# Two elementwise steps of a two-layer attention and MLP kernel move from VectorE to GpSimd, with new GpSimd durations in its planner

## The chip, the cores and the metric

The kernel runs on one core of a Trainium2 chip. The metric is the device time in microseconds (us). A core has five engines that run on their own and meet at semaphores: TensorE (PE in the profile, PEld for its weight loads), ScalarE (ACT), VectorE (DVE), GpSimd (POOL) and SyncE (SP, which issues the DMA transfers). Each engine runs its instructions in a fixed order.

## What is computed

Two rounds of the same pair of blocks, on 2048 tokens of 512 features, all in bfloat16. The first block is softmax attention with 32 heads of 16 features; the second is an MLP with 1376 hidden features and GELU. Each has a layer norm ahead of it and a residual around it.

```python
def _A_ref(x, wqkv, wo):
    H = 32; Dh = D // H
    q, k, v = qkv[0], qkv[1], qkv[2]
    scores = jnp.einsum("bhqd,bhkd->bhqk", q, k) * Dh ** -0.5
    p = _softmax(scores, axis=-1)
    o = jnp.einsum("bhqk,bhkd->bhqd", p, v)
    return o.transpose(0, 2, 1, 3).reshape(B, S, D) @ wo
...
x = A_x
x = x + _A_ref(_layernorm(x), A_wqkv, A_wo)
x = x + _B_ref(_layernorm(x), B_w1, B_b1, B_w2, B_b2)
x = x + _A_ref(_layernorm(x), A_wqkv, A_wo)
x = x + _B_ref(_layernorm(x), B_w1, B_b1, B_w2, B_b2)
```

## The kernel before

**Tiles.** The code calls the two attention blocks `L == 1` and `L == 3`; here they are the first and the second layer. A layer's queries are cut into units (`qc`): four of 512 tokens in the first layer; three of 512 and two of 256 in the second. Heads are taken in eight groups of four (`hg`). A segment is one unit with one head group. Its scores are computed as tiles of 128 keys by 512 queries, for one head each: 16 key blocks times 4 heads is 64 tiles. The first unit of each layer is done in two parts, since its keys are not all there at first: its segments are twice as many and shorter, and their parts are joined afterwards. There are 88 segments and, counted as 128x512, 4096 tiles.

**Scores to output.** For every tile PE multiplies keys and queries into a PSUM bank (L1470), some engine takes the exponential, and PE multiplies the result with the values (L1658), adding into one bank, `ACCB`; the values have a column of ones, so the sum of the exponentials comes out as a 17th row. There are two ways to the exponential. ACT does it on three or two banks at once (L1455, into `PT`). DVE does it by a bit trick: it adds a constant to the score and writes it as a 16-bit integer whose bits are read as bfloat16 (L1555, PSUM to `dp`), and then makes three shifted copies, two tiles at a time (L1588, `dp` to `dp`, in SBUF); each of the four goes through its own product with a weighted copy of the values (`vs`). Only 5 of the 16 key blocks (`DK`) may go DVE's way.

**End of a segment** (`job_segend`). DVE transposes the 17 rows from PSUM into one of two buffers `accT` (L1688) and takes the reciprocal of the denominators, `rv` (L1714). Then `ob`, the part of the output that belongs to this head group, is the product of `accT` and `rv` (L1723, on DVE). In the first unit of a layer, GpSimd first joins the two parts (L1701 in the first part, L1709 to L1712 in the second). When the eight segments of a unit are through, `ob` is transposed by DMA and goes on to the output projection, the MLP and, in the first layer, to the layer norm and the q, k and v of the second (`job_post`, `job_ffn`, `job_lnqkv`).

**Squares.** The softmax uses no maximum but a bound, from the norms of the queries and of the keys. `job_qkv_tile` therefore squares q and k of each token tile (L991) and sums the squares (L1015). In the first layer the squares of k for twelve tiles are done by GpSimd, the rest by DVE. In the second layer DVE squares q and k of a tile together, 128x1024 elements. The bound of a query is then worked out in five small steps by GpSimd (L1029 to L1033).

**What else GpSimd does.** It scales the queries of a segment (`QT`, L1196), makes the weighted values (`vs`, L1221), applies some layer norms (L891) and their small steps (L881 to L886).

**The order.** Nothing is ordered by hand. The Python program plays the whole kernel through before it is built: jobs hand tasks to `Sched`, each with a priority, the tiles that it reads and writes, and a duration in microseconds; `Sched` takes for each engine the best task that is ready and puts it at the end of that engine's stream. How many tiles go DVE's way comes out of this: `take_d` hands DVE a tile when its planned work is small enough. The planned durations thus set the order and the split, and the real ones decide what it costs. For some GpSimd operations the planner also adds a delay to the L1588s beside them (the last number of a task, 0.09 to 0.38). `Hint` holds six thresholds of the planner and a string, `ORDER`, that picks one of ten settings of them for every eight groups of tiles. At last `refill` puts products with zeros (L1359, L1361, L1363) into gaps of PE[...].

Of the kernel before, what the change touches and what calls it, by code (L numbers as in the profile page):

```python
# [14 lines left out]
ALU = mybir.AluOpType  # L15
# [492 lines left out]
class Hint:  # L508
    BASE = dict(D_IDLE=1.2, PV_LEAST=0.75, HOLD_LATE=0.4, PV_NEAR=0.7, LIN2=9, D_STEAL=0)
    MODES = (dict(), dict(D_IDLE=0.8), dict(D_IDLE=1.7), dict(PV_LEAST=0.6), dict(PV_LEAST=0.9), dict(HOLD_LATE=0.2), dict(HOLD_LATE=0.6), dict(PV_NEAR=0.4), dict(LIN2=0.9), dict(D_STEAL=1.0))  # L510
    STEP = 8
    ORDER = '0355550015621021500127723542380000551183094330404202738042440023535555121020004212005090903453421320027044075009578104471100282939255971103200420580357499912000'

    def mode(self, k):
        self.__dict__.update(self.BASE)
# [10 lines left out]
class Builder:  # L526
# [341 lines left out]
    def ln_group(self, tiles, slot, prio, eps1, eps0, shift):  # L868

        for i, tt in enumerate(tiles):  # L870
            c = 4 * slot + i
            s = yield ("get", "st")
            yield Task("dve", prio, [I(lambda e, s=s, tt=tt: e.bn_stats(out=self.st[:, s, :], in_=self.xres[:, tt, :]), [("x", tt)], [("st", s)], 0.65)])
            yield Task("dve", prio - 0.3, [I(lambda e, s=s, c=c: e.bn_aggr(out=self.mv[:, c, :], in_=self.st[:, s, :]), [("st", s)], [("mv", c)], 0.172)])
            self.S_.release("st", s)
        n = len(tiles)
        c0 = 4 * slot
        rs = self.rs[:, c0:c0 + n]
        var = self.mv[:, c0:c0 + n, 1]
        R = ("rs", slot)  # L880
        yield Task("pool", prio, [I(lambda e: e.tensor_scalar(out=rs, in0=var, scalar1=eps1, scalar2=eps0, op0=ALU.mult, op1=ALU.add), [("mv", c0 + i) for i in range(n)], [R], 0.2),  # L881
                                  I(lambda e: e.tensor_tensor(out=rs, in0=rs, in1=self.cneg[:, 0:n], op=ALU.pow), [R, ("cneg",)], [R], 0.45 + 0.15 * n)])
        if shift:
            nmr = self.nmr[:, c0:c0 + n]
            yield Task("pool", prio, [I(lambda e: e.tensor_tensor(out=nmr, in0=self.mv[:, c0:c0 + n, 0], in1=rs, op=ALU.mult), [R] + [("mv", c0 + i) for i in range(n)], [("nmr", slot)], 0.2),
                                      I(lambda e: e.tensor_scalar(out=nmr, in0=nmr, scalar1=-1.0, scalar2=None, op0=ALU.mult), [("nmr", slot)], [("nmr", slot)], 0.2)])  # L886

    def ln_apply(self, tt, slot, i, dst, dres, prio, eng="dve"):
        c = 4 * slot + i
        if eng == "pool":  # L890
            return Task("pool", prio, [I(lambda e: e.tensor_scalar(out=dst, in0=self.xres[:, tt, :], scalar1=self.rs[:, c:c + 1], scalar2=self.nmr[:, c:c + 1], op0=ALU.mult, op1=ALU.add),  # L891
                                         [("x", tt), ("nmr", slot), ("rs", slot)], [dres], 0.92, (), 0.09)])
        return Task("dve", prio, [I(lambda e: e.tensor_scalar(out=dst, in0=self.xres[:, tt, :], scalar1=self.mv[:, c, 0:1], scalar2=self.rs[:, c:c + 1], op0=ALU.subtract, op1=ALU.mult),
                                    [("x", tt), ("mv", c), ("rs", slot)], [dres], 0.395, (), "fast")])

# [20 lines left out]
    def job_qkv_tile(self, L, tt, slot, i, left, prio, what):  # L916
# [12 lines left out]
        qs = yield ("get", "qk")  # L929
# [57 lines left out]
        N = h1 - h0  # L987
        SR = [("sq", ss, k) for k in range(k0, k1)]
        sq = self.sqs(ss)[:, h0:h1, :]
        eng = "pool" if what == "kv" else "dve"  # L990
        yield Task(eng, prio, [I(lambda e: e.tensor_tensor(out=sq, in0=v4, in1=v4, op=ALU.mult), [("qk", qs, k) for k in range(k0, k1)], SR, 0.14 + 0.00845 * N if eng == "dve" else 1.04)])  # L991
        if "k" in what:
            yield Task("dve", prio, [self.norms(self.n2k[:, tt, :], ("n2k", tt), ss, 1)])
            S_.mark(("n2k", L, tt))
# [28 lines left out]
    def bound(self, x, y, a, c, ns, dst, RQ, RN, prio, eng):  # L1023

        yi, y = y.bitcast(I32), y.bitcast(F32)
        RA, RC, RY = ("qt1", ns), ("qt2", ns), ("qy", ns)
        pool = eng == "pool"
        yield Task("dve", prio, [I(lambda e: e.tensor_scalar(out=yi, in0=x.bitcast(I32), scalar1=-0.5, scalar2=RSQRT_MAGIC, op0=ALU.mult, op1=ALU.add), RN, [RY], 0.18)])
        yield Task(eng, prio, [I(lambda e: e.tensor_tensor(out=a, in0=x, in1=y, op=ALU.mult), RN + [RY], [RA], 0.25 if pool else 0.2)])  # L1029
        yield Task(eng, prio, [I(lambda e: e.tensor_tensor(out=c, in0=a, in1=y, op=ALU.mult), [RA, RY], [RC], 0.25 if pool else 0.2)])  # L1030
        yield Task(eng, prio, [I(lambda e: e.tensor_scalar(out=c, in0=c, scalar1=-0.5, scalar2=1.5, op0=ALU.mult, op1=ALU.add), [RC], [RC], 0.217 if pool else 0.2)])
        yield Task(eng, prio, [I(lambda e: e.tensor_tensor(out=a, in0=a, in1=c, op=ALU.mult), [RA, RC], [RA], 0.25 if pool else 0.2)])
        yield Task(eng, prio, [I(lambda e: e.tensor_scalar(out=dst, in0=a.rearrange("p (n o) -> p n o", o=1), scalar1=-MARG, scalar2=0.0, op0=ALU.mult, op1=ALU.add),  # L1033
                                    [RA], [RQ], 0.333 if pool else 0.2)])

    def job_first_tile(self, tt, slot, i, left, prio):

# [105 lines left out]
    def job_scl(self, L, part, prio):  # L1143

        S_ = self.S_
        n = 16 if part == 1 else (4 if L == 1 else 12)
        k = (L // 2) * 2 + part
        n0 = 0
        if n == 16:
            n0 = 12  # L1150
            yield ("keys", [("n2k", L, tt) for tt in range(n0)])
            yield Task("dve", 2.5, [I(lambda e: e.tensor_reduce(out=self.n2k[:, 16, :], in_=self.n2k[:, 0:n0, :].rearrange("p t h -> p h t"), axis=AX.X, op=ALU.max), [("n2k", tt) for tt in range(n0)], [("n2k", 16)], 0.1 + 0.034 * n0)])
        ts = list(range(n0, 17 if n0 else n))
        yield ("keys", [("consts",)])
        yield ("keys", [("n2k", L, tt) for tt in range(n)])
        s = yield ("get", "kmx")
        yield Task("dve", prio, [I(lambda e: e.tensor_reduce(out=self.nm[:, :], in_=self.n2k[:, ts[0]:ts[-1] + 1, :].rearrange("p t h -> p h t"), axis=AX.X, op=ALU.max), [("n2k", tt) for tt in ts], [("nm",)], 0.1 + 0.034 * len(ts))])
        b = yield ("get", "mb")
        yield Task("pe", prio, [I(lambda e, b=b: e.transpose(self.psbf(b)[0:32, 0:128], self.nm[:, :], self.ident[:, :]), [("nm",), ("ident",)], [("ps", b)], 0.1)])
        yield Task("dve", prio, [I(lambda e, b=b: e.tensor_reduce(out=self.kmx[:, 0:1], in_=self.psbf(b)[0:32, 0:128], axis=AX.X, op=ALU.max), [("ps", b)], [("kmx", 0)], 0.2)])  # L1160
        S_.release("mb", b)
        yield Task("pool", prio, [I(lambda e: e.tensor_tensor(out=self.kmx[:, 1:2], in0=self.kmx[:, 0:1], in1=self.chalf[0:32, :], op=ALU.pow), [("kmx", 0), ("chalf",)], [("kmx", 1)], 0.55)])
        yield Task("dve", prio, [I(lambda e: e.tensor_scalar(out=self.krhs[:, :], in0=self.mask8[:, :], scalar1=self.kmx[:, 1:2], scalar2=None, op0=ALU.mult), [("kmx", 1), ("mask8",)], [("krhs",)], 0.1)])
        b = yield ("get", "mb")
        yield Task("pe", prio, [I(lambda e, b=b: e.matmul(self.ps[:, b, 0:8], lhsT=self.sel[:, :], rhs=self.krhs[:, :], start=True, stop=True), [("sel",), ("krhs",)], [("ps", b)], 0.08)])
        yield Task("dve", prio, [I(lambda e, b=b: e.tensor_scalar(out=self.scl[:, k, :], in0=self.ps[:, b, 0:8], scalar1=self.onesm[:, 0:1], scalar2=None, op0=ALU.add), [("ps", b), ("onesm",)], [("scl", k)], 0.15)])
        S_.release("mb", b)
        S_.release("kmx", s)
        S_.mark(("scl", L, part))
# [511 lines left out]
    def job_segend(self, sg):  # L1681
# [33 lines left out]
        if L == 3 and qc == len(self.units[3]) - 1 and hg == 7:  # L1715
            ob = self.obl[:, :].rearrange("p (b r) -> p b r", r=32)
            yield Task("dve", 1.2, [I(lambda e: e.tensor_tensor(out=ob[:, :, 0:16], in0=T[:, :, 0:16], in1=rv.unsqueeze(2).broadcast_to([128, nb, 16]), op=ALU.mult), [RA, ("rv", a)], [("obl",)], 0.147 + 0.268 * W / 512)])
            S_.release("accT", a)
            yield Task("dve", 1.2, [I(lambda e: e.transpose(self.OT[:, 7, 0:W], self.obl[:, 0:W]), [("obl",)], [("OT", 7)], 0.17 + 0.53 * W / 512)])
        else:  # L1720
            if self.prev(L, qc):
                yield ("keys", [("obt",) + self.prev(L, qc)])
            yield Task("dve", 1.2, [I(lambda e: e.tensor_tensor(out=self.ob[:, 0:nb, hg, :], in0=T[:, :, 0:16], in1=rv.unsqueeze(2).broadcast_to([128, nb, 16]), op=ALU.mult), [RA, ("rv", a)], [("ob", hg)], 0.147 + 0.268 * W / 512)])  # L1723
            S_.release("accT", a)
        S_.mark(("ot", L, qc, hg))
        if L == 1 and qc == self.NC - 1:
# [292 lines left out]
```

## Time and profile before

The time is 1564.23 us, the median of three runs (1563.62 to 1565.77). The profiled execution spans 1564.7 us.

| Engine | Busy, us | Share of the span |
|---|---|---|
| PE | 1517.7 | 97% |
| ACT | 1517.1 | 97% |
| DVE | 1459.9 | 93% |
| POOL | 321.2 | 21% |

The largest groups: ACT's exponentials (L1455) 1433.7 us in 1273 instructions; DVE's first step (L1555) 638.1 us in 960, its shifted copies (L1588) 559.9 us in 1452. The multiplication that is moved (L1723) takes DVE 27.6 us in 71 instructions; the squares of the second layer (L991, 128x1024) 11.0 us in 16.

How to read the profile: a group's line has the source line, engine and operation, what is written and read with its shape, the count, then the busy time and the mean of one, and then the idle time of the engine just before these instructions and what ended it. An engine overlaps the end of one instruction with the start of the next, so that counts times means come out above busy times. In a table by windows the columns behind the length are the busy times of PE, PEld, DVE, ACT and POOL, each with its count, the granted clock of PE, and the share and GB/s of the DMA engines.

### The profile page before, as it was taken

The numbers are of one execution on the slowest core, as the hardware profiler recorded it, in microseconds if no ns is written. First come the engines' busy times: TensorE is split into PE (matmuls) and PEld (weight loads), VectorE is DVE, ScalarE is ACT, GpSimd is POOL, SyncE is SP. The second block draws the span as 40 slices with busy tenths as digits, with TensorE's granted clock in tenths as the row PEclk, the third lists the DMA queues.
The fourth block names the chain that finished last, engine by engine and source line by source line (L and its number), as shares of the span: only waits on it lengthen the run. The fifth ranks groups of instructions, "written<-read, shape, count | busy, mean of one in ns | idle before, by whom it ended". The sixth has DMA issues, their size and how long they took to land.

```text
span 1564.7 us, 39699 instructions
## 1 busy us (share of the span) xinstructions
PE 1517.7 (97%) x16674; PEld 483.1 (31%) x16674; DVE 1459.9 (93%) x3256; ACT 1517.1 (97%) x1361; POOL 321.2 (21%) x558
## 2 busy tenths in 40 slices
PE   9999999999999999999999999999999999999998
PEld 3222222232223222222222322222232232344444
DVE  7699999999999899989999799999899999999894
ACT  8979999999999999999999999999999999999996
POOL 3575312001210021203222227410001000020100
PEclk9999999999999999999999999999999999999999
DMA  7663111203311232223832232310102000211110
GB/s 162 116 143 97 35 31 32 61 17 85 85 40 46 47 76 59 61 48 92 145 45 66 56 82 63 62 25 22 35 16 44 22 17 25 41 45 32 43 30 19
DMA packets 212451, 88.69 MB, mean 57 GB/s; under 512 B 183307, under 2 KB 207152, under 8 KB 212272
## 3 DMA queue, kind: packets, MB, share of 16 engines
q1 hardware_dynamic: 212272, 86.16, 24.9%
q8 instruction: 130, 2.13, 0.6%
q14 instruction: 49, 0.40, 0.1%
HBM read 34.65 MB, written 19.48 MB: 35 GB/s over the span
## 4 chain that ended last, share of the span: by engine, by line
ACT 34%; DVE 33%; PE 29%; issue 2%; POOL 1%; SPq 1%; DMA 1%; POOLq 0%; DVEq 0%
ACT PT L1455 33%; DVE dp L1555 13%; DVE dp L1588 10%; PE ps L1470 9%; PE ps L1658 8%; PE ps L1835 3%; PE ps L1792 2%; PE ps L950 2%; DVE accT L1688 2%; DVE n L1015 1%; ACT h L1827 1%; PE ps L1359 1%; DVE sq L991 1%; DVE h L1816 1%; PE ps L1068 1%
## 5 line engine op out<-in xcount | busy, mean ns | idle before, releaser
L1455 ACT ACTIVATE PT<-ps 128x1536 bf16<-128x1536 f32 (+1 forms) x1273 | 1433.7, 1285 | 28.5 <-PE ps L1470 25.1
L1555 DVE TENSOR_SCALAR dp<-ps 128x512 uint16<-128x512 f32 x960 | 638.1, 679 | 36.7 <-PE ps L1470 34.2
L1470 PE MATMUL ps<-QT,KT 32*128 32x512 bf16 (+1 forms) x4608 | 599.1, 359 | 19.6 <-ACT PT L1455 6.8
L1588 DVE TENSOR_SCALAR dp<-dp 128x1024 uint16<-128x1024 uint16 (+1 forms) x1452 | 559.9, 427 | 4.6 <-PE ps L1658 1.6
L1658 PE MATMUL ps<-PT,V 128*17 128x512 bf16 (+1 forms) x3525 | 483.8, 358 | 0.2 <-ACT PT L1455 0.2
L1658 PE MATMUL ps<-dp,vs 128*17 128x512 bf16 (+1 forms) x3249 | 467.6, 357 | 0.9 <-DVE dp L1588 0.4
L1470 PEld LDWEIGHTS ps<-QT,KT 32*128 32x128 bf16 x4608 | 161.1, 91 | 545.9 <-ACT PT L1455 286.3
L1196 POOL TENSOR_SCALAR QT<-qraw,scl,qbias 128x512 bf16<-128x512 bf16 (+1 forms) x83 | 72.3, 872 | 764.6 <-PE ps L1470 758.1
L1658 PE MATMUL ps<-dp,V 128*17 128x512 bf16 (+1 forms) x1083 | 227.1, 358 | 1.6 <-DVE accT L1688 0.6
L1363 PE MATMUL ps<-zw 128*32 128x448 bf16 (+23 forms) x1808 | 172.2, 321 | 0.8 <-DVE dp L1555 0.7
L1658 PEld LDWEIGHTS ps<-dp,vs 128*17 128x17 bf16 x3249 | 119.1, 88 | 115.4 <-issue 87.2
L1658 PEld LDWEIGHTS ps<-PT,V 128*17 128x17 bf16 x3525 | 116.9, 88 | 92.8 <-issue 78.5
L1361 PE MATMUL ps<-zw 32*128 32x444 bf16 (+5 forms) x465 | 132.8, 317 | 0.0
L1359 PE MATMUL ps<-zw 128*128 128x448 bf16 (+17 forms) x487 | 114.7, 334 | 3.2 <-DVE onec L754 2.1
L1792 PE MATMUL ps<-yT,wf 128*128 128x512 bf16 (+3 forms) x396 | 101.7, 361 | 3.1 <-DVE dp L1588 1.3
L950 PE MATMUL ps<-wqkv,xnT 128*128 128x512 bf16 x336 | 93.4, 382 | 5.8 <-DVE dp L963 2.2
L1363 PEld LDWEIGHTS ps<-zw 128*32 128x32 bf16 x1808 | 62.5, 95 | 27.8 <-DVE dp L1555 4.6
L1658 PEld LDWEIGHTS ps<-dp,V 128*17 128x17 bf16 x1083 | 55.5, 88 | 41.4 <-issue 24.1
L1221 POOL TENSOR_SCALAR vs<-V 128x340 bf16<-128x340 bf16 (+2 forms) x72 | 61.8, 859 | 26.1 <-PE ps L1658 15.1
L1688 DVE STREAM_TRANSPOSE accT<-ps 128x512 f32<-128x512 f32 (+1 forms) x88 | 57.8, 657 | 7.1 <-PE ps L1658 7.0
L1816 DVE TENSOR_SCALAR h<-ps,b1c 128x512 bf16<-128x512 f32 (+2 forms) x88 | 61.9, 703 | 1.9 <-PE ps L1792 1.5
L1359 PEld LDWEIGHTS ps<-zw 128*128 128x128 bf16 x487 | 37.6, 98 | 64.7 <-issue 40.0
(182 smaller groups left out, 885.5 us busy)
## 6 DMA issues: line engine op xcount, KB each, us to landing
vs<-vs_scr SPq DMA_DIRECT2D x56, 255.0 KB, 2.7
wf<-in_B_w_dram SPq DMA_DIRECT2D x90, 128.0 KB, 2.9
q_scr<-qk SPq DMA_DIRECT2D x20, 256.0 KB, 2.1
k_scr<-qk SPq DMA_DIRECT2D x12, 256.0 KB, 2.0
out_dram<-xres SPq DMA_DIRECT2D x16, 128.0 KB, 1.8
vs_scr<-vs SPq DMA_DIRECT2D x8, 255.0 KB, 2.9
xres<-in_A_x_dram SPq DMA_DIRECT2D x7, 256.0 KB, 3.2
v_scr<-vst SPq DMA_DIRECT2D x12, 136.0 KB, 1.7
```

What stands on the lines that cost most here:

```text
L950: yield Task("pe", prio if c0 == 0 else min(prio, HINT.LIN2), [I(lambda e, c=c: e.matmul(self.ps[:, b, :], lhsT=xnT[:, c, :], rhs=self.wqk ...
L1359: fn = lambda e: e.matmul(self.ps[:, b, 0:w], lhsT=self.zw[:, 0:128], rhs=self.zw[:, 0:w], start=st, stop=st, skip_group_check=True)
L1361: fn = lambda e: e.matmul(self.ps[:, b, 0:w], lhsT=self.zw[32 * p:32 * p + 32, 0:128], rhs=self.zw[32 * p:32 * p + 32, 0:w], start=st, sto ...
L1363: fn = lambda e: e.matmul(self.ps[32 * p:32 * p + 32, b, 0:w], lhsT=self.zw[:, 0:32], rhs=self.zw[:, 0:w], start=st, stop=st, skip_group_c ...
L1455: S_.submit(Task("act", 1e-5 * gi, [I(lambda e, pt=pt, n=n, b0=b0: e.activation(out=self.PT[:, pt:pt + n, :], in_=self.ps[:, b0:b0 + n, :] ...
L1470: return [I(lambda e, kb=kb, i=i: e.matmul(self.ps[:, b, i * W:(i + 1) * W], lhsT=self.KT[32 * hp:32 * hp + 32, hg, kb * 128:(kb + 1) * 12 ...
L1555: self.S_.submit(Task("dve", 0.0, [I(lambda e: e.tensor_scalar(out=self.dp[:, u, w * 512:(w + 1) * 512], in0=self.ps[:, b, :], scalar1=BIT ...
L1588: yield Task("dve", pr, [I(lambda e, k=k, v=v: e.tensor_scalar(out=self.dp[:, v, 0:N], in0=self.dp[:, u, 0:N], scalar1=float(SHIFT[k]), sc ...
L1658: ops.append((nth[j, sh] + 0.1 * i, I(lambda e, hp=hp, v=v, ap=ap[:, i * W:(i + 1) * W], first=first and i == 0, W=W: e.matmul(self.ps[32 ...
L1688: yield Task("dve", 0.3, [I(lambda e: e.transpose(self.accT[:, a, 0:W], self.ps[:, ACCB, 0:W]), [("ps", ACCB)], [RA], 0.17 + 0.535 * W / 5 ...
L1792: yield Task("pe", pr if c0 == 0 else min(pr, HINT.LIN2), [I(lambda e, c=c: e.matmul(self.ps[0:M, b, off:off + W], lhsT=self.w1(fc, c), rh ...
L1816: S_.submit(Task("dve", pr - 0.7, [I(lambda e, fc=fc, M=M, b=b: e.tensor_scalar(out=hv[0:M, fc * W:(fc + 1) * W], in0=self.ps[0:M, b, 0:W] ...
```

## The change

The multiplication by the reciprocal denominators, L1723 (L1724 after the change), goes to GpSimd, all but the two of the last unit for head groups 5 and 6 (head group 7 of that unit has a line of its own, L1717, and stays on DVE). The squares of the second layer go to GpSimd for the twelve token tiles below 12. Both are meant to free DVE, which is then to take more of the exponentials. The planner gets durations for GpSimd's small operations that are nearer to those of the trace, and the string `ORDER` is another one.

```diff
-    ORDER = '0355550015621021500127723542380000551183094330404202738042440023535555121020...'
+    ORDER = '500550000942402210717323201145450083900431778210649440584538550402055502101004...'
...
-        ... op0=ALU.mult, op1=ALU.add), [("mv", c0 + i) for i in range(n)], [R], 0.2),
-        ... in1=self.cneg[:, 0:n], op=ALU.pow), [R, ("cneg",)], [R], 0.45 + 0.15 * n)])
+        ... op0=ALU.mult, op1=ALU.add), [("mv", c0 + i) for i in range(n)], [R], 0.28),
+        ... in1=self.cneg[:, 0:n], op=ALU.pow), [R, ("cneg",)], [R], 0.58 + 0.15 * n)])
...
-        eng = "pool" if what == "kv" else "dve"
-        ... SR, 0.14 + 0.00845 * N if eng == "dve" else 1.04)])
+        eng = "pool" if what == "kv" or L == 3 and tt < 12 else "dve"
+        ... SR, 0.14 + 0.00845 * N if eng == "dve" else 1.04 * N / 32)])
...
-            yield Task("dve", 1.2, [I(lambda e: e.tensor_tensor(out=self.ob[:, 0:nb, hg, :], in0=T[:, :, 0:16], in1=rv.unsqueeze(2).broadcast_to([128, nb, 16]), op=ALU.mult), [RA, ("rv", a)], [("ob", hg)], 0.147 + 0.268 * W / 512)])
+            late = L == 3 and qc == len(self.units[3]) - 1 and hg > 4
+            yield Task("dve" if late else "pool", 1.2, [I(lambda e: e.tensor_tensor(out=self.ob[:, 0:nb, hg, :], in0=T[:, :, 0:16], in1=rv.unsqueeze(2).broadcast_to([128, nb, 16]), op=ALU.mult), [RA, ("rv", a)], [("ob", hg)], 0.147 + 0.268 * W / 512 if late else 0.1 + 0.58 * W / 512)])
```

The other GpSimd durations changed: layer norm's shift 0.2 and 0.2 to 0.24 and 0.43, its application 0.92 to 0.99; the bound's five steps 0.25, 0.25, 0.217, 0.25, 0.333 to 0.34, 0.26, 0.27, 0.29, 0.45; the square root of the key bound 0.55 to 0.7.

More of the change, by code (lines that the diff above doesn't have):

```diff
@@ L511 @@
     STEP = 8
-    ORDER = '0355550015621021500127723542380000551183094330404202738042440023535555121020004212005090903453421320027044075009578104471100282939255971103200420580357499912000'
+    ORDER = '500550000942402210717323201145450083900431778210649440584538550402055502101004030404145325972120344000190229570058123013000773000079300003010022814735200804803'
     def mode(self, k):
@@ L880, in ln_group @@
         R = ("rs", slot)
-        yield Task("pool", prio, [I(lambda e: e.tensor_scalar(out=rs, in0=var, scalar1=eps1, scalar2=eps0, op0=ALU.mult, op1=ALU.add), [("mv", c0 + i) for i in range(n)], [R], 0.2),
-                                  I(lambda e: e.tensor_tensor(out=rs, in0=rs, in1=self.cneg[:, 0:n], op=ALU.pow), [R, ("cneg",)], [R], 0.45 + 0.15 * n)])
+        yield Task("pool", prio, [I(lambda e: e.tensor_scalar(out=rs, in0=var, scalar1=eps1, scalar2=eps0, op0=ALU.mult, op1=ALU.add), [("mv", c0 + i) for i in range(n)], [R], 0.28),
+                                  I(lambda e: e.tensor_tensor(out=rs, in0=rs, in1=self.cneg[:, 0:n], op=ALU.pow), [R, ("cneg",)], [R], 0.58 + 0.15 * n)])
         if shift:
             nmr = self.nmr[:, c0:c0 + n]
-            yield Task("pool", prio, [I(lambda e: e.tensor_tensor(out=nmr, in0=self.mv[:, c0:c0 + n, 0], in1=rs, op=ALU.mult), [R] + [("mv", c0 + i) for i in range(n)], [("nmr", slot)], 0.2),
-                                      I(lambda e: e.tensor_scalar(out=nmr, in0=nmr, scalar1=-1.0, scalar2=None, op0=ALU.mult), [("nmr", slot)], [("nmr", slot)], 0.2)])
+            yield Task("pool", prio, [I(lambda e: e.tensor_tensor(out=nmr, in0=self.mv[:, c0:c0 + n, 0], in1=rs, op=ALU.mult), [R] + [("mv", c0 + i) for i in range(n)], [("nmr", slot)], 0.24),
+                                      I(lambda e: e.tensor_scalar(out=nmr, in0=nmr, scalar1=-1.0, scalar2=None, op0=ALU.mult), [("nmr", slot)], [("nmr", slot)], 0.43)])
     def ln_apply(self, tt, slot, i, dst, dres, prio, eng="dve"):
@@ L891, in ln_apply @@
             return Task("pool", prio, [I(lambda e: e.tensor_scalar(out=dst, in0=self.xres[:, tt, :], scalar1=self.rs[:, c:c + 1], scalar2=self.nmr[:, c:c + 1], op0=ALU.mult, op1=ALU.add),
-                                         [("x", tt), ("nmr", slot), ("rs", slot)], [dres], 0.92, (), 0.09)])
+                                         [("x", tt), ("nmr", slot), ("rs", slot)], [dres], 0.99, (), 0.09)])
         return Task("dve", prio, [I(lambda e: e.tensor_scalar(out=dst, in0=self.xres[:, tt, :], scalar1=self.mv[:, c, 0:1], scalar2=self.rs[:, c:c + 1], op0=ALU.subtract, op1=ALU.mult),
@@ L989, in job_qkv_tile @@
         sq = self.sqs(ss)[:, h0:h1, :]
-        eng = "pool" if what == "kv" else "dve"
-        yield Task(eng, prio, [I(lambda e: e.tensor_tensor(out=sq, in0=v4, in1=v4, op=ALU.mult), [("qk", qs, k) for k in range(k0, k1)], SR, 0.14 + 0.00845 * N if eng == "dve" else 1.04)])
+        eng = "pool" if what == "kv" or L == 3 and tt < 12 else "dve"
+        yield Task(eng, prio, [I(lambda e: e.tensor_tensor(out=sq, in0=v4, in1=v4, op=ALU.mult), [("qk", qs, k) for k in range(k0, k1)], SR, 0.14 + 0.00845 * N if eng == "dve" else 1.04 * N / 32)])
         if "k" in what:
@@ L1028, in bound @@
         yield Task("dve", prio, [I(lambda e: e.tensor_scalar(out=yi, in0=x.bitcast(I32), scalar1=-0.5, scalar2=RSQRT_MAGIC, op0=ALU.mult, op1=ALU.add), RN, [RY], 0.18)])
[L1029 to L1032, printed above, removed]
+        yield Task(eng, prio, [I(lambda e: e.tensor_tensor(out=a, in0=x, in1=y, op=ALU.mult), RN + [RY], [RA], 0.34 if pool else 0.2)])
+        yield Task(eng, prio, [I(lambda e: e.tensor_tensor(out=c, in0=a, in1=y, op=ALU.mult), [RA, RY], [RC], 0.26 if pool else 0.2)])
+        yield Task(eng, prio, [I(lambda e: e.tensor_scalar(out=c, in0=c, scalar1=-0.5, scalar2=1.5, op0=ALU.mult, op1=ALU.add), [RC], [RC], 0.27 if pool else 0.2)])
+        yield Task(eng, prio, [I(lambda e: e.tensor_tensor(out=a, in0=a, in1=c, op=ALU.mult), [RA, RC], [RA], 0.29 if pool else 0.2)])
         yield Task(eng, prio, [I(lambda e: e.tensor_scalar(out=dst, in0=a.rearrange("p (n o) -> p n o", o=1), scalar1=-MARG, scalar2=0.0, op0=ALU.mult, op1=ALU.add),
-                                    [RA], [RQ], 0.333 if pool else 0.2)])
+                                    [RA], [RQ], 0.45 if pool else 0.2)])
     def job_first_tile(self, tt, slot, i, left, prio):
@@ L1161, in job_scl @@
         S_.release("mb", b)
-        yield Task("pool", prio, [I(lambda e: e.tensor_tensor(out=self.kmx[:, 1:2], in0=self.kmx[:, 0:1], in1=self.chalf[0:32, :], op=ALU.pow), [("kmx", 0), ("chalf",)], [("kmx", 1)], 0.55)])
+        yield Task("pool", prio, [I(lambda e: e.tensor_tensor(out=self.kmx[:, 1:2], in0=self.kmx[:, 0:1], in1=self.chalf[0:32, :], op=ALU.pow), [("kmx", 0), ("chalf",)], [("kmx", 1)], 0.7)])
         yield Task("dve", prio, [I(lambda e: e.tensor_scalar(out=self.krhs[:, :], in0=self.mask8[:, :], scalar1=self.kmx[:, 1:2], scalar2=None, op0=ALU.mult), [("kmx", 1), ("mask8",)], [("krhs",)], 0.1)])
```

## The prediction

> **What bounds the kernel now.** I read the page's totals first, then the busy time of each engine by query unit (the windows end where a unit's last `ob` multiplication starts), then what ScalarE (ACT, whole run) and VectorE (DVE, between 160 and 1525 us) waited for, then the groups by shape, and last the timeline where GpSimd (POOL) and DVE meet.
>
> ```profile
> PE 1517.7 (97%) x16674; PEld 483.1 (31%) x16674; DVE 1459.9 (93%) x3256; ACT 1517.1 (97%) x1361; POOL 321.2 (21%) x558
> ...
> 423.00:608.00 185.00, 182.44 (x1807) 53.34 (x1795) 178.59 (x396) 184.31 (x161) 26.64 (x49) 1.00 0.24 57
> 608.00:797.00 189.00, 185.63 (x1846) 54.90 (x1847) 183.75 (x403) 185.16 (x161) 37.49 (x54) 1.00 0.37 77
> ```
>
> ACT is nearly full and DVE close behind. In the two units shown (first layer, qc 2 and 3; the columns after the length are PE, PEld, DVE, ACT, POOL) ACT is idle 0.7 and 3.8 us, DVE 6.4 and 5.2 us. PE is as busy, but it has about 420 us of L1359, L1361 and L1363, which are filler products with zeros, so it is not the bound. POOL is idle four fifths of the time: its work is free unless it disturbs others.
>
> ```profile
> ACT PT L1455 <- PE ps L1470: 25.1, 47, 6.3
> ...
> DVE dp L1555 <- PE ps L1470: 29.8, 48, 2.1
> ...
> L1455 ACT ACTIVATE PT<-ps 128x1536 bf16<-128x1536 f32 x590 | 893.9, 1515 | 20.2 <-PE ps L1470 17.3
> L1455 ACT ACTIVATE PT<-ps 128x1024 bf16<-128x1024 f32 x683 | 731.8, 1086 | 8.3 <-PE ps L1470 7.7
> L1555 DVE TENSOR_SCALAR dp<-ps 128x512 uint16<-128x512 f32 x960 | 638.1, 679 | 36.7 <-PE ps L1470 34.2
> L1588 DVE TENSOR_SCALAR dp<-dp 128x1024 uint16<-128x1024 uint16 x1428 | 555.0, 430 | 4.6 <-PE ps L1658 1.6
> ```
>
> The exponentials of 4096 score tiles (128x512) are split: ACT does 590x3 + 683x2 = 3136 of them, DVE 960 by its bit trick. So DVE time that comes free can buy tiles from ACT, and ACT time is nearly the kernel's time. Pieces overlap in time: in the trace consecutive starts lie 1.331 us (three tiles) and 0.904 us (two tiles) apart on ACT, 0.601 us for L1555, 0.335 for L1588 at 1024 and 0.202 at 512. I use these distances below, since they are what an engine really spends. One tile on DVE costs 0.601 + 1.5 x 0.335 = 1.10 us.
>
> ```profile
> L1723 DVE TENSOR_TENSOR ob<-accT,rv 128x256 bf16<-128x256 f32 x56 | 23.4, 419 | 0.0
> ...
> L1723 DVE TENSOR_TENSOR ob<-accT,rv 128x128 bf16<-128x128 f32 x15 | 4.2, 281 | 0.0
> ...
> L1709 POOL TENSOR_TENSOR OT<-OT,dw 128x256 f32<-128x256 f32 x16 | 10.7, 667 | 24.4 <-ACT dw L1708 24.4
> L1712 POOL TENSOR_TENSOR accT<-accT,OT 128x256 f32<-128x256 f32 x16 | 12.0, 748 | 1.3
> ...
> L991 POOL TENSOR_TENSOR sq<-h x2: 1041/1042/1042, 56.8 to 80.4; 128x512 bf16<-128x512 bf16 x2
> ...
> 186.93 0.68 DVE L1555 TENSOR_SCALAR dp<-ps 128x512 uint16<-128x512 f32 x1
> 187.53 0.96 DVE L1588 TENSOR_SCALAR dp<-dp 128x1024 uint16<-128x1024 uint16 x1
> ...
> 187.48 0.73 POOL L1712 TENSOR_TENSOR accT<-accT,OT 128x256 f32<-128x256 f32 x1
> ```
>
> The last three lines carry the danger. An L1588 that starts 0.05 us after a two-input GpSimd operation takes 0.96 us instead of 0.42, while the L1555 beside it, which reads PSUM, keeps its 0.68.
>
> [...] L1588s blocked by an L1709 all run on from 0.485 us after it began (of its 0.62), those blocked by an L1712 from about 0.60 us (of 0.73). It also shows the other direction: an L1196 on POOL took 2.11 us behind five L1588s in a row, 0.77 without. [...]
>
> **The change part by part.** The counts come from comparing the two programs' instruction streams.
>
> 1. *Removed from DVE*: 56 `ob` multiplications at 512 queries (0.332 us apart in starts), 13 at 256 (0.199), 12 squares of 128x1024 (0.599): 18.6 + 2.6 + 7.2 = 28.4 us. The last two of the last unit stay (`late`).
> 2. *Added to DVE*: the scheduler spends the room on 16 more tiles: 976 L1555, 1443 + 42 L1588. 16 x 0.601 + 15 x 0.335 + 18 x 0.202 = 18.3 us.
> 3. *Removed from ACT*: 584 triples and 684 pairs, so -6 x 1.331 + 1 x 0.904 = -7.1 us. This is the gain. By unit, first layer qc 2 and 3 get 6 tiles more each, second layer qc 1 4 more, the rest within 2 of before.
> 4. *Added to POOL*: 56 x 0.7 + 13 x 0.4 + 12 x 2.08 (twice the 512 row) = 69 us, on an engine with 1240 us idle. Hidden as work.
> 5. *The lock*. In 40 of the 71 cases the DVE instruction after the reciprocal is an L1588. [...] Summing, for every L1709, how much the DVE instructions beside it exceeded their undisturbed median gives 0.22 us per operation; for L1712 0.27, for single-input bf16 L891 0.14. I take 0.22 for `ob` at 512 and half that at 256: 13.7 us. For the squares no such row exists at 1024 elements; two 0.4 us operations met a 512 square late and lost nothing or 0.02. A 2.08 us hold in which a fast instruction comes after some 0.7 us on average could cost over 1.2 us; the lowest is L891's 0.14. I take 0.8, so 9.6 us. Sum 23 us; ends 10 and 45.
> 6. *Net on DVE*: -28.4 + 18.3 + 23 = +13 us, to about 1473. In qc 2: -(8 x 0.332 + 4 x 0.599) + 6 x 1.10 + 8 x 0.22 + 4 x 0.8 = +6.5 us against 6.4 idle. In qc 3 the same against 5.2. These units become DVE-bound and lose most of ACT's 2 x 2.7 us if the lock costs what I take; elsewhere there is room. A late tile does not all show, as DVE work of the post stages can slide. I charge 2.4 of the 5.3 us.
> 7. *The new wait*: `ob` now stands in POOL's fixed order, in 43 of 69 cases behind a `QT` (0.93 us), sometimes before L1709 or L1221. Behind the waiting `ob` are the next `QT` (needed a segment later), and the release of `accT`, of which there are two, so the transposition of the next but one segment waits. Segments last 20 us mostly; only in second layer part 1 (950 to 1000) 4 to 8 us, where POOL is 33.4 of 50 busy and gets 6 more. I charge nothing, at most 2 us.
> 8. *New POOL durations in the planner, new `ORDER`*: these only move instructions. The start (ACT idle 8 us between 80 and 120) and the filler count (108 matmuls fewer with the 48 more P·V products) may go either way: +-4 us, mean nothing.
>
> Sum: 1564.2 - 7.1 + 2.4 = 1559.5.
>
> **Rivals.** (a) *The lock hardly bites*: DVE's extra is at its low end, +0.2 us net, ACT's gain comes in full and some of its 14.1 us of waits in the middle goes: 1564.2 - 7.1 - 3 = 1554. For it: POOL mostly starts behind a running L1588, and two thirds of the kernel is not near DVE's limit. Against: L1709's 0.22 is measured under the same conditions. (b) *The lock eats the gain*: qc 2 and 3 gain nothing (5.3 back), the shorter stages lose another 1: 1563.5, no difference. For it: the sums in 6. (c) *Slower*: squares block for 1.8 us each, `ob` for 0.38 (L1712 beside a fast operation), DVE +35 us net. The planner does not count this, so PE's in-order stream stands at tiles that are late (L1470 already waits 66.7 us for L1555) and ACT runs dry: a third of 35 us beyond the 7.1 gained, 1564.2 - 7.1 + 12 = 1569. Against: DVE has 50 us idle between 160 and 1520.
>
> **How the numbers follow.** Forecast 1559.5: 0.4. (a) 0.2; (b) 0.2; (c) 0.2. Faster by over 0.2% (below 1561.1): the first two, less a little of the first's upper edge: 0.58. Same 0.21, slower 0.21. Range 1550 to 1570: from (a) with 4 us of luck in the order to (c).
>
> **What would show it.** Right: L1455 near 584 + 684 with ACT busy about 7 us less; L1723's successor on POOL at 0.62 to 0.75 us; mean of L1588 up from 430 to about 445 ns; DVE idle in qc 2 and 3 below 3 us. Wrong: L1588's mean unchanged (then a), ACT waits for L1470 above 35 us (then b or c), a longer wait of L1688 or L1658 around 950 to 1000 (then step 7), a stretch of low PE clock, or a start that is longer or shorter by more than 4 us (then step 8).

## The result, and the profile after

The changed kernel takes 1582.2 us (median; 1580.35 to 1582.89), against 1563.92 us beside it: 1.0113 times the time before, 95% interval [1.0095, 1.013]. It is 18 us slower, where 4.7 us faster was forecast, and lies outside the range (1550 to 1570).

First the page of the changed kernel, then its groups by shape, then what ACT waited for in all, and its query units qc 2 and 3 of the first layer (columns as before: length, PE, PEld, DVE, ACT, POOL, PE clock, DMA share, GB/s).

```profile
PE 1502.0 (95%) x16439; PEld 480.0 (30%) x16566; DVE 1477.1 (93%) x3224; ACT 1513.9 (96%) x1356; POOL 377.1 (24%) x639
```

```profile
L1455 ACT ACTIVATE PT<-ps 128x1536 bf16<-128x1536 f32 x584 | 876.5, 1501 | 37.4 <-PE ps L1470 34.7
L1455 ACT ACTIVATE PT<-ps 128x1024 bf16<-128x1024 f32 x684 | 724.7, 1075 | 9.2 <-PE ps L1470 8.6
L1555 DVE TENSOR_SCALAR dp<-ps 128x512 uint16<-128x512 f32 x976 | 647.7, 678 | 38.1 <-PE ps L1470 34.8
L1588 DVE TENSOR_SCALAR dp<-dp 128x1024 uint16<-128x1024 uint16 x1443 | 583.6, 445 | 4.2 <-PE ps L1658 0.7
...
L1724 POOL TENSOR_TENSOR ob<-accT,rv 128x256 bf16<-128x256 f32 x56 | 36.8, 658 | 153.7 <-DVE rv L1714 152.0 <-DVE dw L1707 1.4 <-DMA xnT<-xn 0.3
...
L991 POOL TENSOR_TENSOR sq<-qk 128x1024 bf16<-128x1024 bf16 x12 | 23.1, 1924 | 23.1 <-DVE qk L963 23.1
```

```profile
ACT PT L1455 <- PE ps L1470: 43.3, 77, 5.5
```

```profile
426.00:620.00 194.00, 184.34 (x1791) 51.56 (x1800) 185.65 (x399) 186.59 (x162) 36.65 (x56) 0.98 0.22 53
620.00:812.00 192.00, 182.29 (x1860) 54.30 (x1878) 188.74 (x402) 184.21 (x159) 48.63 (x72) 1.00 0.39 78
```

The work moved as counted: 16 tiles went from ACT to DVE, and ACT is busy 3 us less. DVE is busier than before, by 17 us, though 28 us were taken from it and 18 added. ACT's waits for scores grew by 18 us (25.1 to 43.3); less the 3 us, that is nearly the 15.9 us between the two traces. By unit, from the start of one unit's last transposition (L1688) to that of the next, in the two traces and in two of the experiments below:

| Stage | before | changed | e1: squares short | e3: both short |
|---|---|---|---|---|
| layer 1, qc 1 | 187.9 | 189.6 | 185.3 | 184.6 |
| layer 1, qc 2 | 185.7 | 192.7 | 187.1 | 186.2 |
| layer 1, qc 3 | 189.4 | 193.3 | 188.5 | 188.7 |
| all else | 1001.7 | 1005.0 | 1005.6 | 1000.6 |
| span | 1564.7 | 1580.6 | 1566.6 | 1560.1 |

Of the 15.9 us between the two traces, 12.6 lie in three units. Each of the three holds four of the twelve squares. In these units ACT waited 18.7 us for scores, where it had waited 4.7 us before.

This is one square, the sixth and the costliest of the twelve, in the timeline of the changed kernel: first POOL, then DVE, then PE's weight loads and products, then ACT.

```profile
591.67 0.25 POOL L1032 TENSOR_TENSOR qt<-qt 128x32 f32<-128x32 f32 x1
591.88 1.89 POOL L991 TENSOR_TENSOR sq<-qk 128x1024 bf16<-128x1024 bf16 x1
```

```profile
591.48 0.67 DVE L977 CAST vst<-ps 128x512 bf16<-128x512 f32 x1
592.07 2.45 DVE L1588 TENSOR_SCALAR dp<-dp 128x1024 uint16<-128x1024 uint16 x2
594.44 0.67 DVE L1555 TENSOR_SCALAR dp<-ps 128x512 uint16<-128x512 f32 x1
```

```profile
595.17 0.09 PEld L1470 LDWEIGHTS ps<-QT,KT 32*128 32x128 bf16 x1 [1.86 <-DVE dp L1555]
```

```profile
595.17 0.38 PE L1470 MATMUL ps<-QT,KT 32*128 32x512 bf16 x1 [1.57 <-DVE dp L1555]
...
597.14 0.61 PE L1470 MATMUL ps<-QT,KT 32*128 32x512 bf16 x3
```

```profile
589.66 5.76 ACT L1455 ACTIVATE PT<-ps 128x1024 bf16<-128x1024 f32 x5
597.80 2.51 ACT L1455 ACTIVATE PT<-ps 128x1536 bf16<-128x1536 f32 x2 [2.38 <-PE ps L1470]
```

The square starts 0.19 us before an L1588. That L1588 takes 1.99 us, and with the next one 2.45 us, where two undisturbed ones (0.42 us each, starts 0.335 us apart) take about 0.75. Behind them in DVE's order stands an L1555, which takes 0.67 us as elsewhere (the twelve L1555s that ran beside a square took 0.67 to 0.68 us), but comes 1.5 us late, as e1 will show; a score product of PE waits 1.9 us until it has ended and its bank is free (595.11), and everything behind that product in PE's order waits too. The products for the scores that ACT needs next start only at 597.14, and ACT stands for 2.38 us until they are done. By that time such a product takes 0.61 us instead of 0.38: PE's granted clock is at half from 595.9 to 602.7, right after five microseconds in which PE was busy for 3.61.

```profile
590.00:595.00 5.00, 3.61 (x34) 0.82 (x32) 5.00 (x8) 4.93 (x5) 4.07 (x6) 1.00 0.20 54
595.90:602.70 6.80, 6.32 (x38) 0.96 (x38) 4.95 (x12) 3.40 (x3) 1.52 (x5) 0.50 0.01 4
```

The half clock makes this square look worse than the rest, but it is not the cause of the loss. It comes once in this trace, and for about 3.4 us each in the trace of the kernel before (at 1214 us) and in that of the repeated run e9. The one run of the changed kernel whose granted clock was 1.0 took 1580.35 us.

### The profile page after: what moved, and what is told of

It is laid out like the page before. It is cut to its first block, busy times and chain, and to the rows that moved or that the text cites. A ratio compares the mean times of both kernels' runs of the same rounds, so it can differ in the third digit from the quotient of the medians.

```text
span 1580.6 us, 39479 instructions
## 1 busy us (share of the span) xinstructions
PE 1502.0 (95%) x16439; PEld 480.0 (30%) x16566; DVE 1477.1 (93%) x3224; ACT 1513.9 (96%) x1356; POOL 377.1 (24%) x639
## 4 chain that ended last, share of the span: by engine, by line
DVE 38%; PE 30%; ACT 27%; issue 3%; DMA 1%; SPq 1%; POOL 1%; POOLq 0%; another core or an unknown queue 0%; DVEq 0%
ACT PT L1455 24%; DVE dp L1555 15%; DVE dp L1588 14%; PE ps L1470 10%; PE ps L1658 9%; PE ps L1836 4%; PE ps L1793 3%; DVE accT L1688 1%; PE ps L950 1%; ACT h L1828 1%; PE ps L1359 1%; DVE n L1015 1%; DVE st L873 1%; PE ps L1363 1%; PE ps L1068 1%
## 5 line engine op out<-in xcount | busy, mean ns | idle before, releaser
L1455 ACT ACTIVATE PT<-ps 128x1536 bf16<-128x1536 f32 (+1 forms) x1268 | 1430.1, 1271 | 46.6 <-PE ps L1470 43.3
L1555 DVE TENSOR_SCALAR dp<-ps 128x512 uint16<-128x512 f32 x976 | 647.7, 678 | 38.1 <-PE ps L1470 34.8
L1470 PE MATMUL ps<-QT,KT 32*128 32x512 bf16 (+1 forms) x4608 | 612.5, 360 | 27.9 <-DVE dp L1555 13.5
L1588 DVE TENSOR_SCALAR dp<-dp 128x1024 uint16<-128x1024 uint16 (+1 forms) x1485 | 593.8, 441 | 4.4 <-PE ps L1658 0.9
L1658 PE MATMUL ps<-PT,V 128*17 128x512 bf16 (+1 forms) x3507 | 492.2, 359 | 0.0
L1196 POOL TENSOR_SCALAR QT<-qraw,scl,qbias 128x512 bf16<-128x512 bf16 (+1 forms) x83 | 69.4, 837 | 609.8 <-PE ps L1470 602.9
L1363 PE MATMUL ps<-zw 128*32 128x448 bf16 (+22 forms) x1695 | 162.7, 319 | 1.3 <-DVE dp L1555 1.1
L1361 PE MATMUL ps<-zw 32*128 32x444 bf16 (+4 forms) x469 | 135.6, 318 | 0.0
L1359 PE MATMUL ps<-zw 128*128 128x448 bf16 (+18 forms) x434 | 105.5, 338 | 3.9 <-DVE onec L754 2.1
L950 PE MATMUL ps<-wqkv,xnT 128*128 128x512 bf16 x302 | 87.3, 384 | 14.3 <-issue 3.3
L1793 PE MATMUL ps<-yT,wf 128*128 128x512 bf16 (+3 forms) x361 | 92.7, 357 | 6.7 <-issue 3.9
L1724 POOL TENSOR_TENSOR ob<-accT,rv 128x256 bf16<-128x256 f32 (+1 forms) x69 | 42.6, 617 | 199.5 <-DVE rv L1714 197.7
L1688 DVE STREAM_TRANSPOSE accT<-ps 128x512 f32<-128x512 f32 (+1 forms) x88 | 57.8, 657 | 11.8 <-PE ps L1658 11.5
```

The source lines that it names most:

```text
L950: yield Task("pe", prio if c0 == 0 else min(prio, HINT.LIN2), [I(lambda e, c=c: e.matmul(self.ps[:, b, :], lhsT=xnT[:, c, :], rhs=self.wqk ...
L1196: yield Task(eng, 0.4, [I(lambda e: e.tensor_scalar(out=self.QT[:, q, 0:W], in0=src, scalar1=self.scl[:, k, hg:hg + 1], scalar2=self.qbias ...
L1359: fn = lambda e: e.matmul(self.ps[:, b, 0:w], lhsT=self.zw[:, 0:128], rhs=self.zw[:, 0:w], start=st, stop=st, skip_group_check=True)
L1361: fn = lambda e: e.matmul(self.ps[:, b, 0:w], lhsT=self.zw[32 * p:32 * p + 32, 0:128], rhs=self.zw[32 * p:32 * p + 32, 0:w], start=st, sto ...
L1363: fn = lambda e: e.matmul(self.ps[32 * p:32 * p + 32, b, 0:w], lhsT=self.zw[:, 0:32], rhs=self.zw[:, 0:w], start=st, stop=st, skip_group_c ...
L1455: S_.submit(Task("act", 1e-5 * gi, [I(lambda e, pt=pt, n=n, b0=b0: e.activation(out=self.PT[:, pt:pt + n, :], in_=self.ps[:, b0:b0 + n, :] ...
```

## The experiments

Two theories stood against each other. *Lock*, a name for what the traces show between GpSimd and L1588 (0.96 us instead of 0.42 beside an L1712, up to 1.99 us beside a square): GpSimd's new work makes L1588s late, and that delay reaches ACT. *Order*: the new string `ORDER` and the new durations gave instruction streams that are worse in themselves. e1 to e3 and e5 leave the streams of PE, ACT and DVE, the waits and the planned durations of the changed kernel as they are, and alter GpSimd's instructions alone. The edits are shown shortened.

**e1, the squares cut short.**

```diff
-  e.tensor_tensor(out=sq, in0=v4, in1=v4, op=ALU.mult)
+  e.tensor_tensor(out=sq[:, 0:1, :], in0=v4[:, 0:1, :], in1=v4[:, 0:1, :], op=ALU.mult)   # L == 3 and tt < 12
```

> The changed kernel with its instruction streams and waits as they are, but GpSimd's twelve squares of the second layer cut to one head of 16 elements: most squares are left out, so the bound is made of old numbers. Lock theory ([...]in the changed kernel's trace DVE instructions beside a square exceed their medians by 1.09 us each, 13 us in all): 1566 to 1571, with the 10 us that unit qc 2 of the first layer lost come back. Order theory (the new ORDER and durations made a stream that is worse whatever GpSimd costs): 1579 to 1583.

Measured 1568.87 us, 1.0027 times before [1.0019, 1.0035]. 13.3 us come back. At the place shown above, the same instructions of DVE and ACT now stand like this:

```profile
587.00 0.22 POOL L991 TENSOR_TENSOR sq<-qk 128x16 bf16<-128x16 bf16 x1
```

```profile
586.60 0.67 DVE L977 CAST vst<-ps 128x512 bf16<-128x512 f32 x1
587.19 0.94 DVE L1588 TENSOR_SCALAR dp<-dp 128x1024 uint16<-128x1024 uint16 x2
588.05 0.68 DVE L1555 TENSOR_SCALAR dp<-ps 128x512 uint16<-128x512 f32 x1
```

```profile
584.77 5.77 ACT L1455 ACTIVATE PT<-ps 128x1024 bf16<-128x1024 f32 x5
590.77 5.97 ACT L1455 ACTIVATE PT<-ps 128x1536 bf16<-128x1536 f32 x5 [0.23 <-PE ps L1470]
```

The pair takes 0.94 us, and ACT's gap is 0.23 us. Both the delay of the pair and the gap go with the length of the square (0.22 us here, 1.89 us in the changed kernel). PE's granted clock stayed at 1.00 here, so the half-clock stretch is part of what came back, but a small one: runs of both at a granted clock of 1.0 still lie 11 to 13 us apart (1580.35 against 1567.79 to 1569.58).

The two programs have the same 1268 exponentials on ACT in the same order, so their starts can be compared one by one in the two traces. The changed kernel falls behind e1 around the squares alone: by 4.3 us over the first four, by 6.0 over the next four (with the half-clock stretch) and by 4.4 over the last four. Everywhere else the distance changes by less than 0.4 us.

**e2, `ob` cut short; e3, both.**

```diff
-  e.tensor_tensor(out=self.ob[:, 0:nb, hg, :], in0=T[:, :, 0:16], ...
+  e.tensor_tensor(out=self.ob[:, 0:1, hg, :], in0=T[:, 0:1, 0:16], ...
```

> The changed kernel with its streams as they are, but GpSimd's 69 multiplications of ob cut to one block of 16 elements (the rest of the attention output is left out). Lock theory: the 0.20 us of excess per multiplication, 12 us over the kernel, go, but half of it lies where DVE has room: 1573 to 1578. Order theory: 1579 to 1583.

> Both cuts at once, squares and ob of GpSimd: the streams of the changed kernel without the lock. Lock theory: what the planner meant, some 7 us below the kernel before for the 16 tiles that ACT no longer does: 1555 to 1560. Order theory: 1576 to 1582. If it ends at 1562 to 1570, both share.

Both also clear `ob` once at the start, with one more GpSimd instruction (1.8 us at 29 us), as most of it is no longer written; whether the zeros in it change anything else was not tested. e2: 1575.41 us, 1.0057 [1.0042, 1.0072], 6.8 us back. e3: 1562.05 us, 0.9978 [0.9967, 0.9988], 20.2 us back. The two add up (13.3 + 6.8), though by the intervals each difference is uncertain by some 3 us. This is what e3's page and its waits of ACT show:

```profile
PE 1514.2 (97%) x16566; PEld 478.5 (31%) x16566; DVE 1455.0 (93%) x3224; ACT 1509.4 (97%) x1356; POOL 334.0 (21%) x640
...
ACT PT L1455 <- PE ps L1470: 28.5, 53, 5.5
```

So the changed kernel's own streams would be 2.7 us faster than before if GpSimd's moved work were as short as in e3. That is less than was expected (1555 to 1560), and just inside the band in which both theories were to share: ACT is busy 7.7 us less than before, but waits 28.5 us for scores instead of 25.1. The order theory, as a cause of the loss, falls with e3: these streams, unchanged, are not slow. That they gain so little stays open.

**e4, the kernel before with the new `ORDER` alone.**

```diff
-    ORDER = '0355550015621021500127723542380000551183...'
+    ORDER = '500550000942402210717323201145450083900...'
```

> The kernel before with the new string ORDER alone, nothing moved to GpSimd. Lock theory: a string that was not chosen for this kernel costs a little, 1564 to 1570. Order theory: the string carries the loss, 1575 to 1585.

Measured 1609.5 us, 1.028 [1.0263, 1.0298]: 45 us slower, beyond what both theories said. The same string gave streams that are not slow with its own durations and tasks (e3), so it is not bad in itself; it does not fit these. Undoing a part of this change and planning again with the same string therefore says little about the part, and the later runs that plan anew have a string searched for each.

**e5, each square in four pieces.**

```diff
-  e.tensor_tensor(out=sq, in0=v4, in1=v4, op=ALU.mult)
+  [e.tensor_tensor(out=sq[:, p:p + 16, :], in0=v4[:, p:p + 16, :], in1=v4[:, p:p + 16, :], op=ALU.mult) for p in range(0, 64, 16)][-1]
```

> The changed kernel with its streams and waits as they are, but each of GpSimd's twelve squares done as four instructions of 16 heads (128x256) one after the other; nothing is left out. If the length of one hold is what hurts: a blocked L1588 waits for the end of one piece, at most some 0.4 us, instead of up to 1.7, the excess per square falls from 1.09 us to 0.3 to 0.6, and the time to 1571 to 1577. If what hurts is that GpSimd's results come late: four pieces take longer than one (about 2.5 us for 1.92), 1582 to 1586. [...]

Measured 1576.53 us, 1.0077 [1.0061, 1.0094]: 5.7 us back, although a square now takes GpSimd longer (four pieces of 0.71 us on average). That the squares' result comes later is therefore not what costs, and in the changed kernel's trace no wait of DVE for a moved square shows. How long one instruction of GpSimd lasts is what costs. Here the fourth square's pieces and the L1588s beside them alternate:

```profile
416.57 2.87 POOL L991 TENSOR_TENSOR sq<-qk 128x256 bf16<-128x256 bf16 x4 [0.46 <-DVE qk L963]
...
417.01 1.96 DVE L1588 TENSOR_SCALAR dp<-dp 128x1024 uint16<-128x1024 uint16 x3
```

Of the 22 L1588s that were held up by over 0.2 us, 14 take 0.83 us and none more, where beside a whole square one took up to 1.99 us. But a square now blocks about two of them: the excess per square is 0.73 us, less than 1.09, and more than the 0.3 to 0.6 that was expected. In sum that is 8.7 us, and e5 is 7.7 us slower than e1.

**e6 to e8, planned anew.** All three keep the new durations of GpSimd's small operations and got a string by the same search in the planner. e6 has squares and `ob` on DVE; e7 has `ob` on GpSimd; e8 has both. e7 and e8 tell the planner of the delay, by the number that delays the L1588s beside an operation, and plan the moved operations a little shorter than the changed kernel did:

```diff
-  ... else 0.1 + 0.58 * W / 512)])
+  ... else 0.1 + 0.56 * W / 512, (), None if late else 0.28 * W / 512)])      # e7, e8
-  ... else 1.04 * N / 32)])
+  ... else 0.03 + 0.95 * N / 32, (), 0.7 * N / 64 if eng == "pool" and L == 3 else None)])      # e8
```

> Squares and ob back on VectorE, with the new GpSimd durations kept and a string ORDER searched for afresh in the planner (the same search for e6, e7 and e8). Lock theory: 1560 to 1567, as the kernel before[...]. Order theory (the changed kernel is slow because its string and durations are worse): 1575 or more.

> ob on GpSimd, squares on VectorE, and the planner told of the lock (an L1588 beside an ob takes 0.28 us longer), ORDER searched for afresh. Lock theory: what the planner knows it can place around: 1560 to 1568. If the loss comes from something that a plan can't see (GpSimd's queue, accT held longer): 1570 or more.

> The changed kernel with both parts on GpSimd, but the planner told of the lock: 0.28 us for an L1588 beside an ob, 0.7 us beside a square; ORDER searched for afresh. Lock theory: 14 to 22 us below the changed kernel, 1558 to 1567. If a square on GpSimd costs more than it frees however it is placed: 1570 or more.

> The changed kernel once more, on the chip of e6 to e8, as their base: 1580 to 1584.

| Run | Time, us | Ratio to before | Tiles on DVE |
|---|---|---|---|
| e6, nothing moved | 1566.53 | 1.0014 [1.0007, 1.002] | 964 |
| e7, `ob` moved | 1567.08 | 1.0014 [1.0008, 1.0021] | 965 |
| e8, both moved | 1574.92 | 1.0063 [1.0048, 1.0078] | 975 |
| e9, the changed kernel | 1582.26 | 1.0111 [1.0096, 1.0126] | 976 |

With nothing moved, a string of its own and the new durations, the time is within 0.2% of before: the new durations are harmless. `ob` on GpSimd is then neither gain nor loss: e7 equals e6, and the freed DVE time buys one tile. The squares are a loss even when the planner counts the delay: e8 is 7.8 us slower than e7. It missed the 1558 to 1567 of the lock theory as I had put it, and fell where a square costs more than it frees however it is placed. Eleven of its twelve squares still blocked an L1588, and the DVE instructions beside a square exceeded their medians by 1.07 us on average, so the planner did not keep L1588s clear of the squares. The 7.3 us between e8 and the changed kernel belong to what the planner was told and to the new string together; the two were not separated. Each of these runs is one string, and the luck of a string was not measured. No version ran faster than the kernel before with all of the work done.

## Why the prediction was wrong

*Steps 1 to 4* (counts, ACT's busy time, GpSimd's added work) held. In e3, where GpSimd's moved work is cut short, ACT is busy 1509.4 us against 1517.1, 7.7 us less for the 7.1 worked out. GpSimd's durations were 0.66, 0.44 and 1.92 us for 0.7, 0.4 and 2.08.

*Step 5* (the lock) had nearly the sizes. Summed in the same way, the DVE instructions beside an `ob` exceed their medians by 0.20 us (0.22 taken) and 0.07 at 256 queries (0.11), beside a square by 1.09 us (0.8 taken). All twelve squares blocked an L1588; at nine it runs on 1.76 us after the square began, at three, where the square itself began behind an L1588, 1.87 to 1.94 us after. The sum is 25 us for 23.

*Step 6's net on DVE* held too: 1477.1 us busy for "about 1473".

*Step 6's last sentence* is the one that failed: "A late tile does not all show, as DVE work of the post stages can slide. I charge 2.4 of the 5.3 us." It took the delay as load on DVE, which could at worst eat the gain of two units, and fill DVE's idle time first. Against the 2.4 us charged, e3 puts the cost of the delays at 20.2 us. The runs showed a delay that is passed on: the DVE instructions beside the squares exceed their medians by 13.1 us in sum, and the squares cost 13.3 us of time (e1); beside `ob` it is 12.3 us, for 6.8 us of time (e2). DVE's idle time was not used up first: in the windows of qc 2 and 3 shown with the result DVE is still idle for 8.4 and 3.3 us. It is no cushion, because it does not lie behind the square: L1588 and the L1555 behind it are in a fixed order, and so are PE's products behind the late bank. What ACT had in hand was little: at eleven of the squares its loss against e1 was at most 0.4 us less than the delay of DVE, and at the sixth, with the half clock, it was more. Rival (c) described just this; it was given a third of 35 us, 12 us for 20.2, and a chance of 0.2. The share that is passed on was near one for squares, where L1588 ran on after 1.76 us, and about half, give or take a quarter, for `ob`, where it mostly ran on after 0.53 us. With the measured terms the sum is 1564.2 - 2.7 + 20.2 = 1581.7.

*Steps 7 and 8* (the wait for GpSimd's queue, and the order) were charged nothing. Second layer part 1, the stage with short segments, took 50.9 us for 48.9 before, within the 2 us allowed; 0.7 of them go with the length of `ob` (50.2 in e2 and e3). e3 keeps the order, and the queue with shorter work in it, and only 2.7 of the 7.1 us arrived there. How the missing 4.4 us divide between step 7, step 8 and other waits is not shown. As a general size for an order, "+-4 us" was far off: a string that doesn't fit costs 45 us (e4).

Of the signs named ahead, L1588's mean rose from 430 to 445 ns as forecast, and ACT's waits above 35 us pointed to (b) or (c). But ACT was busy only 3 us less instead of 7, and DVE's idle time in qc 2 and 3 did not fall below 3 us. The stretch of low PE clock was meant to point to step 8; it is absent in e1, which has the same order.

## What to carry to other kernels

When an instruction of one engine makes those of another late, as a square on GpSimd did with L1588 (1.99 us instead of 0.42), work moved from the second to the first is not free because the first is idle: ask how long one instruction of it lasts, and what stands behind the instruction that it delays. Here an `ob` at 512 queries took 0.33 us of work from DVE and put 0.2 us of delay on it; a square took 0.6 us and put 1.1 us on it. A delay in a fixed order is not load: compare it with the slack of the next engine in the chain (here at most 0.4 us at a square), not with the idle time of a stage. And where a planner decides the order, give it the delay as well as the duration, and never judge a part by planning again with settings chosen for the whole.

## What the runs showed of the hardware that was not expected

Blocked L1588s ran on (their end, less their undisturbed 0.42 us) 1.76 us after the start of a square of 1.89 us, and 1.94 us after one of 2.07, 0.13 us before its recorded end in both cases. Whether a square itself ended at its recorded end is not shown, and so neither is whether L1588 ran on before it.

Which of the two engines went on next was not the same everywhere. In e5, with pieces queued on GpSimd and L1588s queued on DVE, the two alternated one by one at most places, each L1588 0.83 us long beside a piece. In the changed kernel a square that began while an L1588 ran took 2.07 us instead of 1.89, with no second L1588 right behind that one; in e8 a square took 2.34 us beside two in a row, and in the kernel before an L1196 took 2.11 us beside five, where its median is 0.77. What decides it is not shown.

PE's granted clock fell to half for 6.8 us after five microseconds in which PE was 72% busy (3.61 of 5 us). In e1, where PE was busier there (14.52 of 15 us from 585 to 600), it stayed at 1.00. No threshold follows from this: in the changed kernel's trace PE was busy for only 3.24 us from 115 to 120, and the clock stayed at 1.00.
